# First 1/rms by ln and exp on ScalarE, squares shared with GpSimd, 128-column score weights, first projections in parts, last store split

## Chip, cores, metric

One core of one Trainium2 chip. The metric is the device time of one execution in microseconds (us). Several executions are taken of each kernel. "Clock" is the mean TensorE clock that the throttle granted, with 1.0 as full speed.

## The reference

Attention with normalised q and k, then a gated two-layer projection (shapes: 8 batches, 12 heads, 448 positions, head size 64; model width 768, hidden width 2048):

```python
def rmsnorm(x, g):
    rms = np.sqrt(np.mean(x * x, axis=-1, keepdims=True) + 1e-06)
    return x / rms * g
q_n, k_n = rmsnorm(q, g_q), rmsnorm(k, g_k)
scores = scale * np.matmul(q_n, k_n.transpose(0, 1, 3, 2))     # then softmax
attn_out = np.matmul(attn, v)
x = attn_out.transpose(0, 2, 1, 3).reshape(B * S, H * D)
h = x @ w_in
out = (h * (1.0 / (1.0 + np.exp(-1.702 * h)))) @ w_out
```

## The kernel before

Heads go in 48 pairs. A pair is loaded, squared (ACT), summed (DVE), given 1/rms (a bit-trick seed and two Newton steps), multiplied by it ("norm"), turned on PE, copied out of PSUM by DVE, scored in four chunks, exponentiated (ACT), multiplied with v on PE, divided (DVE), turned back and copied to `xt`. Six pairs make one batch's input of the first projection. A list scheduler written into the kernel emits the instructions; where it sees PE idle early on, it emits filler matmuls on zeros, meant to keep the clock up (before's trace shows full clock from 6.6 us, where its record of the clock begins, to 443.5). Each engine then runs its own list in that order, so an instruction waits behind whatever stands before it (on PE a transposition of pair 6 waits for GpSimd until 47.69 us, and pair 5's values, whose last exponential ended at 45.22, follow at 47.90).

```python
groups = [[0], [1, 2], [3, 4, 5]] + [list(range(j, j + 3)) for j in range(NP, NG, 3)]
def fill(idle):
    for _ in range(int(idle * FILL / 110)):
        nc.tensor.matmul(banks[2][:, :256], lhsT=ident[:, :], rhs=zeros[:, :], start=True, stop=True)
def square(i, part):
    ...
    nc.scalar.activation(out=sq_of[i][:SS, part], in_=raw[i][:SS, part], func=ACT.Square)
def rsqrt(grp):
    eng = nc.vector if grp[0] == 0 else nc.gpsimd
    ...                                   # two Newton steps
def norm(i, gi):
    eng = nc.vector if i == 0 else nc.gpsimd
    ...
def score(i, kcs):
    for kc in kcs:
        ...
            nc.tensor.matmul(sc[:SS, hp, :S], lhsT=qk_ring[i % N_KZ][r, 1, kc, :],   # 112 columns
                             rhs=qk_ring[i % N_KZ][r, 0], start=True, stop=True)
def first(b, m):                          # waits for all six pairs of the batch
    ...
    for ki in range(KI):
        nc.tensor.matmul(ps, lhsT=w_in_s[:, ki, m * 128:(m + 1) * 128],
                         rhs=xT[b][:, ki, :], start=(ki == 0), stop=(ki == KI - 1))
```

Of the kernel before, what the change touches and what calls it, by code (L numbers as in the profile page):

```python
# [19 lines left out]
class _Task:  # L20
    __slots__ = ("eng", "dur", "lat", "emit", "key", "after", "at", "takes", "left", "users", "end", "start", "lock", "widen", "moves", "rest", "there")


class _Order:
# [3 lines left out]
    def __init__(self):  # L28
        self.tasks = []
        self.named = {}  # L30
        self.slots = {}
        self.fill = None

# [3 lines left out]
    def add(self, name, eng, dur, emit, key, deps=(), lat=100.0, at=0.0, takes=None,  # L37
            lock=False, widen=None, moves=None):

        t = _Task()  # L40
        t.eng, t.dur, t.lat, t.emit = eng, dur, lat, emit
        t.after, t.at, t.takes = tuple(deps), AT.get(name, at), takes
        t.users, t.end, t.lock, t.widen = [], None, lock, widen
        t.moves = moves
        t.key = KEYS.get(name, key)
        self.tasks.append(t)
        self.named[name] = t

    def run(self):
# [53 lines left out]
        while emitted < len(self.tasks):  # L103
            for eng, q in ready.items():
                while q and free[eng] <= now:
# [12 lines left out]
                    if best.takes:  # L118
                        self.slots[best.takes[0]][1].extend(best.takes[1])
# [13 lines left out]
                    if best.moves:  # L133
                        best.rest, best.there, best.end = best.moves, free[eng] + 1500.0, 1e12
# [30 lines left out]

    def _fits(self, t, now):
# [3 lines left out]
        if not t.takes:  # L170
            return True
        n, held = self.slots[t.takes[0]]
# [9 lines left out]
KEYS = {  # L182
    ('V', 6): 2.73, ('KQ', 4): 2.03, ('O', 6, 0): 3.05, ('O', 6, 1): 3.05, ('N', 6, 0): 1.73,
    ('N', 6, 1): -2.28, ('Q0', 5): 5.11, ('X', 5): 3.87, ('O', 4, 0): 10.58, ('O', 4, 1): 10.58,
    ('V', 9): -3.51, ('B', 4): 5.7, ('N', 8, 0): 9.82, ('N', 8, 1): 17.49, ('R', 7, 0): -27.36,
    ('C', 5, 0): -2.3, ('C', 5, 1): -2.05, ('C', 5, 2): -1.8, ('C', 5, 3): -1.55, ('C', 0, 0):
    7.52, ('C', 0, 1): 7.77, ('C', 0, 2): 8.02, ('C', 0, 3): 8.27, ('X', 7): 22.5, ('E', 9, 0):
    1.77, ('E', 9, 1): 2.02, ('E', 9, 2): 2.27, ('E', 9, 3): 2.52, ('E', 8, 0): 9.55, ('E', 8,
    1): 9.8, ('E', 8, 2): 10.05, ('E', 8, 3): 10.3, ('L', 4, 0): -3.71, ('L', 4, 1): -1.78,
    ('L', 4, 2): 3.79, 'gG': 2.03, ('L', 6, 0): 16.21, ('L', 6, 1): 16.04, ('L', 6, 2): 15.02,  # L190
    ('V', 4): 11.79, ('X', 2): 31.45, ('KQ', 6): 7.83, ('O', 2, 0): 1.7, ('O', 2, 1): 1.7, ('O',
    3, 0): 5.2, ('O', 3, 1): 5.2, ('V', 5): -21.45, ('T', 1, 0): -1.19, ('T', 1, 1): -1.19,
    ('B', 8): 8.59, ('K', 0): -8.3, ('P', 8, 0, 0): 6.19, ('P', 8, 0, 1): 6.31, ('P', 8, 0, 2):
    6.44, ('P', 8, 0, 3): 6.56, ('P', 8, 1, 0): 6.69, ('P', 8, 1, 1): 6.81, ('P', 8, 1, 2):
    6.94, ('P', 8, 1, 3): 7.06, ('P', 3, 0, 0): 10.39, ('P', 3, 0, 1): 10.51, ('P', 3, 0, 2):
    10.64, ('P', 3, 0, 3): 10.76, ('P', 3, 1, 0): 10.89, ('P', 3, 1, 1): 11.01, ('P', 3, 1, 2):
    11.14, ('P', 3, 1, 3): 11.26, ('S', 1, 0): -4.92, ('S', 1, 1): -4.92, ('O', 0, 0): -14.63,
    ('O', 0, 1): -14.63, ('X', 0): 0.11, ('R', 2, 0): -12.65, ('B', 6): -4.39, ('B', 0): 6.44,
    ('WI', 1): -46.42, ('T', 6, 0): -14.6, ('T', 6, 1): -14.6, ('KQ', 7): 8.67, ('N', 7, 0):
    0.23, ('N', 7, 1): 0.86, ('WI', 2): -48.21, ('P', 9, 0, 0): 1.73, ('P', 9, 0, 1): 1.85,  # L200
    ('P', 9, 0, 2): 1.98, ('P', 9, 0, 3): 2.1, ('P', 9, 1, 0): 2.23, ('P', 9, 1, 1): 2.35, ('P',
    9, 1, 2): 2.48, ('P', 9, 1, 3): 2.6, ('Q0', 8): 26.56, ('L', 9, 0): 1.37, ('L', 9, 1): 2,
    ('L', 9, 2): 2.03, ('S', 2, 0): 3.28, ('WO', 0): -62.3, ('S', 7, 0): -6.72, ('K', 6): 8.9,
    ('V', 2): 6.1, ('C', 9, 0): 8.24, ('C', 9, 2): 8.74, ('E', 0, 0): 7.69, ('E', 0, 1): 7.94,
    ('E', 0, 2): 8.19, ('E', 0, 3): 8.44, ('R', 3, 0): -4.24, ('K', 3): 15.15, ('K', 4): -25.1,
    ('B', 7): 15.31, ('WI', 3): -42.16, ('T', 9, 0): 1.28, ('T', 9, 1): 1.28, ('E', 5, 0):
    12.03, ('E', 5, 1): 12.28, ('E', 5, 2): 12.53, ('E', 5, 3): 12.78, ('B', 1): -1.87, ('E', 7,
    0): 28.17, ('E', 7, 1): 28.42, ('E', 7, 2): 28.67, ('E', 7, 3): 28.92, ('K', 8): 47.59,
    ('L', 0, 0): -11.05, ('L', 0, 1): -11.4, ('L', 0, 2): -7.53, ('N', 3, 0): -16.28, ('N', 3,
    1): -14.36, ('K', 2): -16.75, ('Q', 0): -4.76, ('Q', 2): -5.74, ('KQ', 0): -29.98, ('T', 3,  # L210
    0): -12.32, ('T', 3, 1): -12.32, ('P', 6, 0, 0): 3.39, ('P', 6, 0, 1): 3.51, ('P', 6, 0, 2):
    3.64, ('P', 6, 0, 3): 3.76, ('P', 6, 1, 0): 3.89, ('P', 6, 1, 1): 4.01, ('P', 6, 1, 2):
    4.14, ('P', 6, 1, 3): 4.26, ('R', 9, 0): 25.96, ('T', 0, 0): 0.39, ('T', 0, 1): 0.39, ('B',
    5): 2.45, ('S', 8, 0): 3.96, ('O', 5, 0): -1.87, ('O', 5, 1): -1.87, ('N', 9, 1): -9.18,
    ('K', 9): 3.37, ('E', 6, 0): 19.35, ('E', 6, 1): 19.6, ('E', 6, 2): 19.85, ('E', 6, 3):
    20.1, ('N', 0, 0): -4.14, ('N', 0, 1): -1.78, ('S', 4, 0): -31.05, ('O', 1, 0): -5.09, ('O',
    1, 1): -5.09, ('N', 1, 0): -9.91, ('N', 1, 1): -1.76, ('V', 7): -0.09, ('KQ', 3): -10.96,
    ('N', 9, 0): -5.62, ('L', 7, 1): -15.12, ('T', 8, 0): 3.81, ('T', 8, 1): 3.81, ('V', 8):
    4.32, ('E', 2, 0): -5.17, ('E', 2, 1): -4.92, ('E', 2, 2): -4.67, ('E', 2, 3): -4.42, ('R',
    4, 0): 6.71, ('R', 6, 0): -1.32, ('P', 5, 0, 0): 16.5, ('P', 5, 0, 1): 16.62, ('P', 5, 0,  # L220
    2): 16.75, ('P', 5, 0, 3): 16.87, ('P', 5, 1, 0): 17, ('P', 5, 1, 1): 17.12, ('P', 5, 1, 2):
    17.25, ('P', 5, 1, 3): 17.37, ('WO', 1): -77.76, ('S', 5, 0): -1.79, ('V', 1): 4.46, ('S',
    0, 0): -28.66, ('S', 0, 1): -28.66, ('B', 2): 9.79, ('Q0', 2): -3.7, ('P', 2, 0, 0): 5.38,
    ('P', 2, 0, 1): 5.51, ('P', 2, 0, 2): 5.63, ('P', 2, 0, 3): 5.76, ('P', 2, 1, 0): 5.88,
    ('P', 2, 1, 1): 6.01, ('P', 2, 1, 2): 6.13, ('P', 2, 1, 3): 6.26, ('K', 1): 5.11, ('KQ', 5):
    -13.6, ('E', 4, 0): -6.4, ('E', 4, 1): -6.15, ('E', 4, 2): -5.9, ('E', 4, 3): -5.65, ('N',
    4, 0): -13.48, ('N', 4, 1): -11.01, ('P', 1, 0, 0): 25.19, ('P', 1, 0, 1): 25.32, ('P', 1,
    0, 2): 25.44, ('P', 1, 0, 3): 25.57, ('P', 1, 1, 0): 25.69, ('P', 1, 1, 1): 25.82, ('P', 1,
    1, 2): 25.94, ('P', 1, 1, 3): 26.07, ('N', 2, 0): 5.89, ('N', 2, 1): 6.22, ('S', 3, 0):
    -13.09, ('R', 5, 0): 13.51, ('S', 9, 0): -6.12, ('KQ', 8): -5.51, ('P', 7, 0, 0): 19.18,  # L230
    ('P', 7, 0, 1): 19.31, ('P', 7, 0, 2): 19.43, ('P', 7, 0, 3): 19.56, ('P', 7, 1, 0): 19.68,
    ('P', 7, 1, 1): 19.81, ('P', 7, 1, 2): 19.93, ('P', 7, 1, 3): 20.06, ('X', 4): 4.14, ('R',
    0, 0): -18.6, ('R', 0, 1): -18.6, ('Q', 8): -19.17, ('B', 9): 2.73, ('E', 1, 0): -9.59,
    ('E', 1, 1): -9.34, ('E', 1, 2): -9.09, ('E', 1, 3): -8.84, ('T', 4, 0): 15.41, ('T', 4, 1):
    15.41, ('WO', 3): -23.99, ('C', 1, 0): -11.21, ('C', 1, 1): -10.96, ('C', 1, 2): -10.71,
    ('C', 1, 3): -10.46, ('L', 5, 0): 3.49, ('L', 5, 1): 4.35, ('L', 5, 2): -1.58, ('Q', 5):
    -7.85, ('X', 1): -14.02, ('T', 2, 0): 0.05, ('T', 2, 1): 0.05, ('C', 6, 0): 3.8, ('C', 6,
    2): 4.3, ('K', 5): -7.73, ('K', 7): -10.83, ('Q0', 0): -13.4, ('KQ', 1): -28.02, ('X', 9):
    -9.97, ('N', 5, 0): 8.49, ('N', 5, 1): 10.13, ('T', 5, 0): 15.04, ('T', 5, 1): 15.04, ('O',
    8, 0): 20.07, ('O', 8, 1): 20.07, ('V', 3): -0.2, ('C', 8, 0): 8.01, ('C', 8, 2): 8.51,  # L240
    ('L', 7, 0): -16.71, ('L', 7, 2): -14.17, ('S', 6, 0): -1.89, ('L', 2, 0): -13.69, ('L', 2,
    1): -12.03, ('L', 2, 2): -10.74, ('L', 8, 0): 3.25, ('L', 8, 1): 8.83, ('L', 8, 2): 15.6,
# [27 lines left out]
def kernel(  # L270
# [37 lines left out]
    zeros = consts.tile([128, 256], BF16)  # L308
    nc.vector.memset(zeros[:, :], 0.0)
    ones = consts.tile([128, 1], FP32)  # L310
    nc.vector.memset(ones[:, :], 1.0)


    gq = consts.tile([128, 1], FP32)
# [325 lines left out]
    def first(b, m):  # L640
        if b == m == 0:
            order.insert(0, 2)
# [123 lines left out]
```

## Time and profile before

| | before |
|---|---|
| median, 3 runs | 448.08 us (447.36 to 448.12) |
| profiled span, clock | 446.0 us, 0.997 |
| first exponential starts, 24th ends | 16.40, 45.22 us |
| first projection starts | 50.77 us |
| last matmul ends | 440.74 us |

A line of a timeline gives start, length, engine, source line, operation, tiles, and in brackets how long the engine was idle before it and what released it. The prediction below shows the lines that carry the argument. One more belongs here, the VectorE timeline where pair 0 is normed:

```profile
13.03 0.69 DVE L439 TENSOR_TENSOR row<-raw,rs 112x512 bf16<-112x512 f32 x1
```

One norm takes 0.69 us on DVE (the other 0.68).

### The profile page before, as it was taken

The page shows a single profiled execution, that of the slowest core. Times are in us where ns is not written, and L with a number is a line of the kernel's source. Part 1 is how long each engine was busy: PE and PEld are TensorE (multiplying, and loading weights), DVE is VectorE, ACT ScalarE, POOL GpSimd, SP SyncE. Part 2 cuts the span into 40 slices and gives each one's busy share as a digit, 9 for nine tenths or more (in the row PEclk, how much of TensorE's full clock was granted, in tenths as well). Part 3 has the DMA queues.
Part 4 walks back from the last instruction along what each step waited for, and adds up shares of the span by engine and source line. Part 5 has one row for each costly group of instructions (what it writes and reads, how often), then busy time and mean ns, then how long its engine had stood idle before and what let it go on. Part 6 is the DMA issues. An engine that isn't in the chain of part 4 may idle for free.

```text
span 446.0 us, 9981 instructions
## 1 busy us (share of the span) xinstructions
PE 437.9 (98%) x3955; PEld 259.2 (58%) x3955; DVE 214.3 (48%) x458; ACT 319.0 (72%) x463; POOL 184.8 (41%) x285
## 2 busy tenths in 40 slices
PE   8999999999999999999999999999999999999995
PEld 6767655665556555565556555565555555565552
DVE  3778777664763347633762256612541125404400
ACT  4689588898998878977887788866876667414311
POOL 1775985656646453544643635455242100000000
PEclk9999999999999999999999999999999999999998
DMA  7999999959556775397456684445123430121022
GB/s 205 274 235 245 262 249 241 225 149 223 149 141 156 189 196 151 83 210 189 122 137 155 178 208 114 125 109 135 32 57 74 105 77 12 22 71 37 0 72 71
DMA packets 97391, 63.38 MB, mean 142 GB/s; under 512 B 54336, under 2 KB 93760, under 8 KB 97344
## 3 DMA queue, kind: packets, MB, share of 16 engines
q1 hardware_dynamic: 89488, 56.22, 50.2%
q0 software_dynamic: 7296, 6.29, 8.7%
q8 instruction: 31, 0.51, 0.5%
q10 hardware_dynamic: 560, 0.23, 0.2%
q14 instruction: 16, 0.13, 0.1%
HBM read 45.61 MB, written 11.01 MB: 127 GB/s over the span
## 4 chain that ended last, share of the span: by engine, by line
PE 87%; DMA 7%; POOL 2%; DVE 2%; SPq 0%; issue 0%; ACT 0%; ACTq 0%; POOLq 0%; DVEq 0%
PE w L668 33%; PE w L645 32%; PE o L498 11%; PE sc L487 9%; DMA raw<-in_q_dram 5%; POOL row L439 1%; DMA gq<-in_g_q_dram 1%; DMA vraw<-in_v_dram 1%; PE w L459 1%; DVE ssq L401 1%; POOL w_in_s L619 0%; PE w L521 0%; SPq L390 0%; DVE rs L414 0%; DVE g L660 0%
## 5 line engine op out<-in xcount | busy, mean ns | idle before, releaser
L491 ACT ACTIVATE att<-sc 112x896 bf16<-112x896 f32 x192 | 167.9, 916 | 22.1 <-PE sc L487 20.9
L668 PE MATMUL w<-w_out_s,g 128*128 128x384 bf16 x896 | 161.6, 326 | 0.0
L645 PE MATMUL w<-xt,w_in_s 128*128 128x448 bf16 x768 | 158.4, 352 | 0.4 <-DVE g L660 0.2
L668 PEld LDWEIGHTS <-g 128*128 128x128 bf16 x896 | 80.3, 97 | 50.9 <-issue 5.7
L660 DVE SCALAR_TENSOR_TENSOR g<-th,w 128x448 bf16<-128x448 f32 x128 | 78.9, 618 | 63.9 <-ACT th L654 63.6
L645 PEld LDWEIGHTS <-w_in_s 128*128 128x128 bf16 x768 | 69.5, 97 | 57.5 <-issue 2.1
L439 POOL TENSOR_TENSOR row<-raw,rs 112x512 bf16<-112x512 f32 x94 | 96.0, 1044 | 16.4 <-DMA qk<-row 14.7
L498 PEld LDWEIGHTS <-att 112*128 112x128 bf16 x1536 | 73.7, 98 | 45.0 <-issue 21.1
L654 ACT ACTIVATE th<-w 128x448 f32<-128x448 f32 x128 | 69.8, 545 | 36.8 <-PE w L645 35.4
L449 POOL TENSOR_TENSOR vx<-vraw,ones 112x512 bf16<-112x512 f32 x42 | 43.7, 1042 | 113.8 <-PE o L498 106.6
L498 PE MATMUL o<-vx,att 112*128 112x65 bf16 x1536 | 87.4, 194 | 0.2 <-DVE obs L509 0.2
L401 DVE TENSOR_REDUCE ssq<-sq 112x16 f32<-112x1024 f32 (+1 forms) x50 | 58.5, 1174 | 28.9 <-ACT sq L395 27.7
L508 DVE RECIPROCAL rcp<-o 112x4 f32<-112x4 f32 x96 | 17.3, 180 | 97.9 <-PE o L498 97.3
L678 ACT ACTIVATE osb<-w 128x384 f32<-128x384 f32 x56 | 27.5, 490 | 50.9 <-PE w L668 49.2
L487 PE MATMUL sc<-qk 64*112 64x448 bf16 x384 | 57.9, 373 | 0.3 <-DVE qk L466 0.2
L395 ACT ACTIVATE sq<-raw 112x1024 f32<-112x1024 f32 (+1 forms) x50 | 51.1, 1023 | 8.9 <-DMA raw<-in_k_dram 8.1
L509 DVE TENSOR_TENSOR obs<-o,rcp 112x256 bf16<-112x256 f32 x96 | 40.7, 424 | 3.3
L369 PE MATMUL w<-zeros,ident 128*128 128x256 bf16 x227 | 32.5, 288 | 1.4 <-POOL ident masks.py:199 1.4
L487 PEld LDWEIGHTS <-qk 64*112 64x112 bf16 x384 | 17.8, 124 | 16.3 <-issue 11.2
L369 PEld LDWEIGHTS <-ident 128*128 128x128 bf16 x227 | 21.7, 103 | 7.0 <-issue 2.3
L477 ACT ACTIVATE qk<-qk,gG 128x448 bf16<-128x448 bf16 x36 | 24.2, 672 | 0.0
L425 POOL TENSOR_TENSOR t<-rs 112x48 f32<-112x48 f32 (+1 forms) x32 | 8.8, 275 | 33.8 <-DVE rs L414 31.1
(32 smaller groups left out, 89.9 us busy)
## 6 DMA issues: line engine op xcount, KB each, us to landing
raw<-in_q_dram SPq DMA_DIRECT2D x48, 224.0 KB, 4.1
vraw<-in_v_dram SPq DMA_DIRECT2D x48, 224.0 KB, 3.9
raw<-in_k_dram SPq DMA_DIRECT2D x47, 224.0 KB, 4.3
w_in_s<-in_moe_w_in_dram POOLq DMA_DIRECT2D x4, 768.0 KB, 14.3
w_out_s<-in_moe_w_out_dram POOLq DMA_DIRECT2D x4, 768.0 KB, 15.7
out_dram<-osb SPq DMA_DIRECT2D x8, 336.0 KB, 3.0
out_dram<-osb SPq DMA_DIRECT2D x8, 288.0 KB, 2.8
out_dram<-osb SPq DMA_DIRECT2D x8, 240.0 KB, 3.3
```

The lines of the kernel that those rows point to most:

```text
L369: nc.tensor.matmul(banks[2][:, :256], lhsT=ident[:, :], rhs=zeros[:, :], start=True, stop=True)
L395: nc.scalar.activation(out=sq_of[i][:SS, part], in_=raw[i][:SS, part], func=ACT.Square)
L401: nc.vector.reduce_sum(out=ssq_of[g0][:SS, i - g0, part], in_=sq_of[i][:SS, part], axis=AX.X)
L439: eng.tensor_tensor(out=row_ring[i % N_QKN][:SS, gi].rearrange("p n (h d) -> p h n d", h=2), in0=raw[i][:SS, gi], in1=y[:SS, a, gi].to_bro ...
L449: nc.gpsimd.tensor_tensor(out=vx[:, :, :D], in0=vr, in1=ones[:SS, :].to_broadcast([SS, 2 * NS, D]), op=ALU.mult)
L487: nc.tensor.matmul(sc[:SS, hp, :S], lhsT=qk_ring[i % N_KZ][r, 1, kc, :], rhs=qk_ring[i % N_KZ][r, 0], start=True, stop=True)
L491: nc.scalar.activation(out=att_ring[i % N_ATT][:SS, kc, :, :S], in_=scs.pop((i, kc))[:SS, :, :S], func=ACT.Exp)
L498: nc.tensor.matmul(os_[i, hp][:, qs, :], lhsT=att_ring[i % N_ATT][:SS, kc, hp, qs * SS:qs * SS + WIN], rhs=vx_ring[i % N_V][:SS, hp, kc, : ...
L645: nc.tensor.matmul(ps, lhsT=w_in_s[:, ki, m * 128:(m + 1) * 128], rhs=xT[b][:, ki, :], start=(ki == 0), stop=(ki == KI - 1))
L654: nc.scalar.activation(out=th[:, :], in_=gps[b, m], func=ACT.Tanh, scale=0.851)
L660: nc.vector.scalar_tensor_tensor(out=g_of[b // 2][:, m, lo:lo + S], in0=ths.pop((b, m))[:, :], scalar=1.0, in1=gps.pop((b, m)), op0=ALU.ad ...
L668: nc.tensor.matmul(ops[bp, tm, hf], lhsT=g_of[bp][:, ko, tm * 128:(tm + 1) * 128], rhs=w_out_s[:, ko, hf * HALF:(hf + 1) * HALF], start=(k ...
```

## The change

The intent: get the attention of the first six pairs out sooner, by taking the Newton steps off DVE and GpSimd (ln and exp on ACT need two short instructions), moving some squares from ACT to GpSimd, and beginning the first two projections with the pairs that are ready; and shorten the dense stage with 128-column score weights. Its core, with cuts; the scheduler's priorities were redrawn as well, and buffers became fixed rings:

```diff
 def square(i, part):
+    if ("S", i, part.start) in ON:
+        nc.gpsimd.tensor_tensor(out=sq[i % N_SQ][:SS, part], in0=raw[...], in1=raw[...], op=ALU.mult)
+        return
...
+def by_log(i):                            # pairs 0 to 5
+    nc.scalar.activation(out=x, in_=x, func=ACT.Ln, bias=eps[:SS, :])
+    nc.scalar.activation(out=y[:SS], in_=x, func=ACT.Exp, scale=-0.5)
...
-    nc.tensor.matmul(sc[:SS, hp, :S], lhsT=qk_ring[i % N_KZ][r, 1, kc, :],
+    k0 = S + kc * SS
+    nc.tensor.matmul(sc[:, hp, :S], lhsT=qkw_ring[i % N_KZ][r, k0:k0 + WIN],      # WIN = 128
...
-def first(b, m):
+def first(b, m, kis):
...
+    parts = [range(KI - 2), [KI - 2], [KI - 1]] if b == 0 and m < 2 else [range(KI)]
...
-    for lo in (0, 64):                    # g loads: from ACT's queue to SP's
-        nc.scalar.dma_start(out=t[lo:lo + 64, :], in_=src.rearrange("(d o) -> d o", o=1))
+    nc.sync.dma_start(out=t[:, :], in_=src.rearrange("(x d o) -> x d o", x=1, o=1).to_broadcast([2, D, 1]))
...
+    for j, eng in enumerate((nc.scalar, nc.vector)):     # the last tile: halves, stores on two queues
```

## The prediction

> **What bounds the kernel now.** I read the page first: engine shares, the slices, then the costliest groups. Lines from the page (engine, busy time; then group: line, engine, operation, busy us, mean ns, idle before):
>
> ```profile
> PE 437.9 (98%) x3955; PEld 259.2 (58%) x3955; DVE 214.3 (48%) x458; ACT 319.0 (72%) x463; POOL 184.8 (41%) x285
> DMA  7999999959556775397456684445123430121022
> ...
> L491 ACT ACTIVATE att<-sc 112x896 bf16<-112x896 f32 x192 | 167.9, 916 | 22.1 <-PE sc L487 20.9
> ...
> L369 PE MATMUL w<-zeros,ident 128*128 128x256 bf16 x227 | 32.5, 288 | 1.4 <-POOL ident masks.py:199 1.4
> L487 PEld LDWEIGHTS <-qk 64*112 64x112 bf16 x384 | 17.8, 124 | 16.3 <-issue 11.2
> L498 PEld LDWEIGHTS <-att 112*128 112x128 bf16 x1536 | 73.7, 98 | 45.0 <-issue 21.1
> ```
>
> PE looks full, but 227 of its matmuls are fillers on zeros (L369). The PE timeline shows where they sit: all are before the first projection (L645) at 50.77 us. The windows view split at that moment and at the last matmul gives:
>
> ```profile
> 0.00:50.77 50.77, 48.48 (x560) 35.59 (x560) 34.43 (x85) 33.77 (x40) 30.74 (x60) 1.00 1.07 241
> 50.77:440.76 389.99, 389.39 (x3398) 223.61 (x3396) 179.89 (x374) 284.71 (x423) 154.06 (x226) 1.00 0.54 130
> ```
>
> So there are two stages. After 50.77 PE is busy 389.4 of 390.0 us with real work: only less PE work can shorten it. Before 50.77, PE waits for the first six head pairs, and ACT sets the pace. The ACT and PE timelines (start, length, engine, what, count):
>
> ```profile
> 1.36 12.97 PE L369 MATMUL w<-zeros,ident 128*128 128x256 bf16 x94 [1.36 <-POOL ident masks.py:199]
> 16.40 0.92 ACT L491 ACTIVATE att<-sc 112x896 bf16<-112x896 f32 x1 [1.79 <-PE sc L487]
> 26.91 3.34 ACT L491 ACTIVATE att<-sc 112x896 bf16<-112x896 f32 x4 [0.40 <-PE sc L487]
> 44.26 0.96 ACT L491 ACTIVATE att<-sc 112x896 bf16<-112x896 f32 x1
> 47.69 0.37 PE L459 MATMUL w<-ident,row 112*128 112x112 bf16 x4 [0.67 <-POOL row L439]
> ```
>
> The first exponential starts at 16.40, the 24th (six pairs, four each) ends at 45.22. These 28.8 us are 24 x 0.835 (3.34/4) = 20.0, seven squares at a pitch of 0.945 = 6.6, and 2.1 of small waits. Then 5.6 us pass to the first projection, partly because a transposition of pair 6 stands in PE's order ahead of pair 5's values and waits for GpSimd until 47.69.
>
> PE time without use before 50.77: 1.36 at the start; 94 fillers up to 14.17 us, 12.8; 133 more x 0.107 = 14.2; idle 1.1. Sum **29.5 us**; so 21.3 us was useful.
>
> [...] 112 columns load in 124 ns, 128 columns in 98, with 112 rows or 128. [...] Here 94 fillers take 12.8 us; at 0.107 they would take 10.0, so some 26 ran at 0.213. [...] The one load here took 1283 ns[...]. [...] Here the 112x512 product takes 1044 ns on POOL, 683 on DVE.
>
> **The change, part by part.** Counts are from the instruction order of the built program.
>
> *1/rms of pairs 0 to 5.* Removed on DVE for pair 0: two seed and six Newton instructions, 8.26 to 9.90 = 1.6 us, with three reductions ahead of the first norm (9.82 to 12.2). Removed on POOL: 16 small instructions for pairs 1 to 5, 13.2 to 16.2 and 23.1 to 26.2, together 6 us, and the wait of a pair for its group. Added on ACT: a ln and an exp of 16 columns per pair. [...] Two pairs are before the first exponential, four after.
>
> *Squares.* Of the squares of full or half pairs, POOL takes two halves (1.04 each) and those of pairs 3, 6, 7, 9, 10, 11 (about 2.1 each). Between first and 24th exponential ACT keeps three squares, 3 x 0.945 = 2.8, instead of seven.
>
> *First exponential.* 57 fillers now precede the first transposition: 26 x 0.213 + 31 x 0.107 = 8.9, so PE is free at 10.2. Pair 0's loads land at about 6 to 6.5 (5.2 and 5.8 before; they now stand behind one more load and the two small g loads); square 0.63, reduction 0.68[...], two norms 1.3: about 10.3. Transposition, copies (0.39 + 0.45), score and semaphores took 2.2 us before (14.16 to 16.40). First exponential: about **12.2** instead of 16.4.
>
> *The 24th.* 20.0 + 2.8[...] + the same 2.1 of waits = 27.1, so 39.3 instead of 45.2.
>
> *First projections in parts.* Ten of the first 12 matmuls (0.19 each) now run before pair 5 is done; after the last exponential come values, division, values, division, transposition, copy: about 4.0 us to the end of the first projection. Useful PE work up to there is the six pairs (48 transpositions at 0.049, 24 scores at 0.33, 48 value groups at 0.13, 6 transpositions back: 17.7) plus 2.3 of projection plus the same 2.4 of switching: 22.4. Time without use: 39.3 + 4.0 - 22.4 = **20.9**.
>
> *The same by counting fillers.* 138 instead of 227: 1.36 + 8.9 + 81 x 0.107 (8.7) + idle. After the first projection begins no filler is placed, and the order shows five waits for DVE round trips (two of about 0.9, the others 0.3 to 0.7), so I take 3 us of idle: **22**. Both ways: 29.5 falls by 7.5 to 8.6. I take **7.8**.
>
> *Score weights.* 84 double steps (four loads each) lie in the dense stage. Each load is 124 - 98 = 26 ns shorter, but loads partly lie beside matmuls. One to two of four exposed: 84 x 0.026 to 0.052 = 2.2 to 4.4. A single look at such a step: second pair of matmuls 0.23 after the first, next operation 0.28 later, where streaming alone is two times 0.187. I take **2.5**.
>
> *Last store.* Before, the last 384 columns leave PSUM in 0.49, then two stores are issued one after the other (0.45 each) from SP. Now half the bytes, issued from two queues: minus 0.45 and an estimated 0.5 of transfer; but the order shows DVE's part waiting for ACT's: plus 0.25. **0.7** saved.
>
> *Neutral.* Free choice of PSUM bank and fixed rings: in the dense stage PE waited 0.4 us in all, so nothing is to be had. The second table load (1.28) follows the 24th exponential and lies under the 4 us of values and divisions.
>
> Sum: 7.8 + 2.5 + 0.7 = 11.0; 448.1 - 11.0 = **437.1**, say 437.0.
>
> **Rivals.** *DMA becomes the bound of the start.* For: its slices are full from 11 to 89 us, and single loads took 8.35 and 12.87 us from issue to landing while weights moved; now three of four input weight chunks are asked for before pair 3 is normed, and two output chunks before pair 4 is. If pair 4 or 5 lands 3 us late, the time is 440. Against: pair 5's last load is the 20th of its queue; twenty of 229 KB at the 247 GB/s of this stretch (0.93 us each) and two or three chunks at 4.9 (8.7% of the span for eight) make some 30 us, and pair 5 is needed at about 26 to 28 us: near need, so not excluded. *GpSimd becomes the bound.* Pair 2's rows stand behind a 2.1 us square; if its lane stalls the exponentials, 1 to 2 us are lost: 438.5. Against: it loses 6 us of Newton steps and gains about as much. *The start is gained but refunded later*: if a gap in the dense stage opens because ACT or POOL is late, the gain shrinks to 6 or 7: 441. Against: ACT is busy 285 of 390 there and POOL 154. *Everything lands*: exposed weight loads at two per step and no idle after the first projection: 433.
>
> **Range and chances.** Main uncertainty: idle in the first 45 us, about 2.5 us either way; weight loads 1 us. Range 433 to 441.5. The 2% line is at 439.1, some 0.8 of my spread away, and a DMA wait is the one likely way across it: faster 0.72, same 0.26, slower 0.02.
>
> **What would show it.** Right: first exponential near 12.2, 24th ends near 39.3, first projection whole near 43, time without use near 21.5; weight loads of scores near 98 ns and the dense PE work 2.5 us shorter; span after the last matmul 4.5 instead of 5.2. Wrong: raw loads of pairs 2 to 5 as the releasers of ACT's squares with long waits; PE idle of over 4 us after the first projection has begun; score steps as long as before in spite of shorter loads; releasers from GpSimd in the dense stage.

Passages of the prediction are cut. With them goes the term for ln and exp, which stood in two sums: 10.3 us for pair 0's norms and 27.1 from the first exponential to the end of the 24th are the sums as recorded, with that term in them, and so are 12.2, 39.3, 20.9 and 437.1, which follow from them. (A ln and an exp took 0.30 and 0.22 us in the changed kernel's trace, started 0.33 apart.) The 0.5 of transfer in the last store's term is the author's estimate; the page of before has a median of 3.0 us from issue to landing for stores of 336 KB and 2.7 for those of 192 KB.

## The result

After: 440.15 us (median of 4 runs, 439.37 to 441.26) against 447.79 for before on the same chip. Ratio 0.983, 95% interval 0.981 to 0.986. The gain is 7.6 us where 11 was predicted, inside the predicted range but 3.1 us above its centre, and on the "within 2%" side of the line.

The page of the changed kernel: engine shares, the granted clock and the DMA share in 40 slices, then the costliest groups.

```profile
PE 428.7 (98%) x3866; PEld 244.6 (56%) x3866; DVE 216.2 (49%) x452; ACT 316.3 (72%) x468; POOL 191.2 (44%) x277
PEclk9899899999999999999999999999999999999999
DMA  7999999594699974677547774655133430121022
...
L433 PE MATMUL w<-zeros,ident 128*128 128x256 bf16 x138 | 22.6, 305 | 1.4 <-POOL ident masks.py:199 1.4
L558 PEld LDWEIGHTS <-qk 64*128 64x128 bf16 x384 | 11.8, 94 | 19.4 <-issue 14.6
```

Score weights now load in 94 ns instead of 124, and there are 138 fillers instead of 227. But the clock row has two eights, in the slices from 11 and from 44 us. Splitting the start where the clock changes gives the windows view (stretch, its length, then busy us and count of PE, weight loads, DVE, ACT, POOL; then clock, DMA share and GB/s):

```profile
0.00:13.24 13.24, 9.54 (x64) 7.25 (x65) 5.68 (x12) 4.54 (x8) 6.59 (x21) 1.00 0.80 203
13.24:16.65 3.41, 3.27 (x19) 1.66 (x19) 1.66 (x3) 0.94 (x2) 3.14 (x3) 0.50 1.11 272
16.65:40.36 23.71, 23.71 (x312) 15.36 (x313) 17.61 (x42) 22.45 (x32) 17.91 (x17) 1.00 1.17 248
40.36:47.34 6.98, 4.65 (x68) 3.06 (x67) 5.34 (x13) 3.11 (x4) 3.80 (x11) 1.00 1.19 246
47.34:50.75 3.41, 3.30 (x9) 1.32 (x9) 1.20 (x3) 1.10 (x3) 3.41 (x4) 0.50 1.22 249
50.75:435.07 384.32, 384.18 (x3398) 216.00 (x3396) 184.35 (x381) 283.83 (x421) 156.35 (x226) 1.00 0.56 133
```

TensorE ran at half speed in two stretches of 3.41 us each, 34.1 us (ten times 3.41) apart. (The 1.00 of the first row holds only from 6.4 us on: the trace records no clock before that, and there the fillers follow each other at 0.213 us instead of 0.107.) Each stretch follows a time in which PE was partly idle. Ahead of the first these were the waits for pair 0, in the PE timeline:

```profile
11.63 0.37 PE L529 MATMUL w<-ident,row 112*128 112x112 bf16 x4 [1.43 <-DVE row L509]
...
13.38 0.53 PE L529 MATMUL w<-ident,row 112*128 112x112 bf16 x4 [1.05 <-DVE qk L533]
```

Before has no such stretch from 8 to 20 or from 40 to 55 us. The dense stage is full, as before: 384.18 of 384.32 us busy.

Pair 0's first steps, from the ACT timeline, then the loads that SP issued:

```profile
7.98 0.63 ACT L458 ACTIVATE sq<-raw 112x512 f32<-112x512 f32 x1 [5.97 <-DMA raw<-in_q_dram]
...
15.71 0.92 ACT L562 ACTIVATE att<-sc 112x896 bf16<-112x896 f32 x1 [2.91 <-PE sc L558]
...
40.46 1.73 ACT L562 ACTIVATE att<-sc 112x896 bf16<-112x896 f32 x2
42.21 1.28 ACT L356 ACT_TABLE_LOAD   x1
```

```profile
0.73 0.39 SPq L451 DMA_DIRECT2D raw<-in_q_dram  x1
1.18 0.72 SPq L608 DMA_DIRECT2D gq<-in_g_q_dram  x1
1.95 0.54 SPq L608 DMA_DIRECT2D gk<-in_g_k_dram  x1
2.53 2.03 SPq L451 DMA_DIRECT2D raw<-in_q_dram  x2
```

Pair 2's q goes first, then both g; pair 0's q is in the pair of loads that took 2.03 us to issue (the single load ahead of them took 0.39, the g loads 0.72 and 0.54), and ACT waits for it until 7.98. The first exponential starts at 15.71, hardly earlier than the 16.40 of before. The 24th ends at 42.19, followed by the table load. Then the VectorE and GpSimd timelines around pair 0's norms:

```profile
10.43 2.59 DVE L509 TENSOR_TENSOR row<-raw,rs 112x512 bf16<-112x512 f32 x2
```

```profile
9.99 1.04 POOL L519 TENSOR_TENSOR vx<-vraw,ones 112x512 bf16<-112x512 f32 x1 [1.69 <-DVE ssq L467]
11.18 2.74 POOL L509 TENSOR_TENSOR row<-raw,rs 112x512 bf16<-112x512 f32 x2 [0.15 <-ACT rs L479]
```

Two norms took 2.59 us on DVE, where two of 0.68 would make 1.36, while GpSimd worked beside them and needed 2.74 for two of its own norms (2.04 in experiments 2, 5 and 12, where it did them after DVE's). Last, the PE timeline after the first parts of the projections:

```profile
43.56 0.37 PE L590 MATMUL w<-ident,obs 112*128 112x112 bf16 x4 [0.99 <-DVE obs L578]
...
45.17 0.68 PE L569 MATMUL o<-vx,att 112*128 112x65 bf16 x16 [0.23 <-DVE obs L578]
46.60 0.37 PE L590 MATMUL w<-ident,obs 112*128 112x112 bf16 x4 [0.74 <-DVE obs L578]
47.45 4.43 PE L725 MATMUL w<-xt,w_in_s 128*128 128x448 bf16 x14 [0.48 <-DVE xt L593]
```

Four waits for DVE, 2.4 us together, with no filler in them; then 14 projection matmuls take 4.43 us at half clock where 14 of 0.19 are 2.7. And the chain of waits that ended last runs through this place so (start, length, what):

```profile
39.63 0.95 ACT sq L458
40.61 2.35 DVE ssq L467 x2
...
43.08 0.44 DVE obs L578
```

The chain isn't that of the last exponentials: it comes from the square of a later pair on ACT (itself behind earlier exponentials), two reductions of later pairs on DVE, and only then pair 4's second division.

The last matmul ends at 435.07 in a span of 439.5: 4.43 us of tail against 5.26 before.

So between the two profiled runs the last matmul moved by 440.74 - 435.07 = 5.67 us and the tail by 0.83. As experiment 9 measures the score weights at 2.7, some 3.0 us are left for the start, where 7.8 was predicted. The question for the experiments is where the other 4.8 went.

### The profile page after: what moved, and what is told of

Same layout as the page of the kernel before. It is cut to its first block, busy times and chain, and to the rows that moved or that the text cites. A ratio compares the mean times of both kernels' runs of the same rounds, so it can differ in the third digit from the quotient of the medians.

```text
span 439.5 us, 9799 instructions
## 1 busy us (share of the span) xinstructions
PE 428.7 (98%) x3866; PEld 244.6 (56%) x3866; DVE 216.2 (49%) x452; ACT 316.3 (72%) x468; POOL 191.2 (44%) x277
## 4 chain that ended last, share of the span: by engine, by line
PE 94%; DVE 2%; DMA 1%; ACT 1%; SPq 1%; issue 0%
PE w L748 34%; PE w L725 33%; PE o L569 12%; PE sc L558 11%; PE w L433 2%; PE w L529 1%; DVE ssq L467 1%; DMA raw<-in_q_dram 1%; PE w L590 1%; SPq L451 0%; ACT att L562 0%; ACT sq L458 0%; DVE row L509 0%; DVE obs L578 0%; SPq L608 0%
## 5 line engine op out<-in xcount | busy, mean ns | idle before, releaser
L509 POOL TENSOR_TENSOR row<-raw,rs 112x512 bf16<-112x512 f32 x90 | 92.8, 1054 | 26.7 <-DMA qk<-row 19.7
L569 PEld LDWEIGHTS <-att 112*128 112x128 bf16 x1536 | 70.9, 98 | 42.8 <-issue 21.2
L569 PE MATMUL o<-vx,att 112*128 112x65 bf16 x1536 | 83.8, 194 | 0.2 <-DVE obs L578 0.2
L467 DVE TENSOR_REDUCE ssq<-sq 112x16 f32<-112x1024 f32 (+1 forms) x50 | 58.1, 1171 | 20.9 <-ACT sq L458 20.8
L558 PE MATMUL sc<-qk 64*128 64x448 bf16 x384 | 55.3, 357 | 0.1
L458 ACT ACTIVATE sq<-raw 112x1024 f32<-112x1024 f32 (+1 forms) x42 | 43.3, 1034 | 7.1 <-DMA raw<-in_q_dram 6.0
L433 PE MATMUL w<-zeros,ident 128*128 128x256 bf16 x138 | 22.6, 305 | 1.4 <-POOL ident masks.py:199 1.4
L558 PEld LDWEIGHTS <-qk 64*128 64x128 bf16 x384 | 11.8, 94 | 19.4 <-issue 14.6
L433 PEld LDWEIGHTS <-ident 128*128 128x128 bf16 x138 | 13.5, 109 | 7.0 <-issue 3.1
L455 POOL TENSOR_TENSOR sq<-raw 112x1024 f32<-112x1024 f32 (+1 forms) x8 | 13.3, 1678 | 6.6 <-DMA raw<-in_k_dram 2.5
```

What stands on the lines that cost most here:

```text
L458: nc.scalar.activation(out=sq[i % N_SQ][:SS, part], in_=raw[i % N_RAW][:SS, part], func=ACT.Square)
L467: nc.vector.reduce_sum(out=ssq_of[g0][:SS, i - g0, part], in_=sq[i % N_SQ][:SS, part], axis=AX.X)
L509: eng.tensor_tensor(out=row_ring[i % N_QKN][:SS, gi].rearrange("p n (h d) -> p h n d", h=2), in0=raw[i % N_RAW][:SS, gi], in1=y[:SS, a, gi ...
L558: nc.tensor.matmul(sc[:, hp, :S], lhsT=qkw_ring[i % N_KZ][r, k0:k0 + WIN], rhs=qk_ring[i % N_KZ][r, 0], start=True, stop=True)
L569: nc.tensor.matmul(os_[i, hp][:, qs, :], lhsT=att_ring[i % N_ATT][:SS, kc, hp, qs * SS:qs * SS + WIN], rhs=vx_ring[i % N_V][:SS, hp, kc, : ...
```

## The experiments

Times are medians. Experiments 1 to 4 shared one set of runs of before (447.67), 5 to 8 another (447.6), 9 to 12 a third (447.91). Where a run is compared with one of another set (5, 7, 8 and 10 with 3, 11 with 1), the difference of the ratios to before gives the same within 0.2 us.

**1. The changed kernel once more, unedited.** It measures how far it repeats.

> The changed kernel once more, unedited, as the base for this chip. Expected 440 us (ratio 0.983 to the kernel before), with a spread of about 2 us from run to run, and in its trace again half-clock stretches near 14 and 47 us. If the half-clock stretches are an accident of the one profiled run, they are missing here.

440.86 us (439.32 to 442.04, 5 runs), ratio 0.984. A stretch of 3.41 us at half speed lowers the mean clock by 3.41 x 0.5 / 440 = 0.0039, so the mean clock counts the stretches of a run, but roughly: the clock can also fall after the last matmul (in before's trace from 443.5 us on, which alone makes its 0.997). Of the nine runs of the changed kernel, five have clock 0.992, two stretches, and take 441.2 us in the mean; four have 0.994 to 0.996, about one, and take 439.7. The spread of 2.7 us follows this count. This run's own trace has the two again, at 13.64 and 47.77, once more 34.1 apart.

**2. Fillers in the four waits after the 24th exponential**, 20 in all, that add zero to the open projection:

```diff
+def warm(n):
+    for _ in range(n):
+        nc.tensor.matmul(gps[0, 0][:, :256], lhsT=ident[:, :], rhs=zeros[:, :], start=False, stop=False)
 def values(i, hp, qs):
+    if (i, hp, qs) == (5, 1, 0): warm(2)
 def back_pe(i):
+    if i in (4, 5): warm(8 if i == 4 else 6)
 ...                                       # and warm(4) ahead of the first projection's last part
```

> 20 matmuls on zeros, which add nothing, are put into the four waits of TensorE between the first part of the first projection and its last part. Clock theory: the granted clock stays 1.00 from 40 to 52 us, the 14 projection matmuls at 47.5 us take 2.7 us instead of 4.4, and the kernel gets 1.5 to 1.8 us faster than the unedited one, in those runs that had the drop. Rival (only the DVE round trips bound this stretch, the drop is harmless): same time within 0.4 us.

440.73 us (437.67 to 441.33), ratio 0.983. The one traced run had no half-clock stretch (clock 0.999), its 14 projection matmuls took 2.93 us, and it was the fastest, 437.67. The four others had 0.992 to 0.994 and were no faster than without the fillers. They have no trace, so where they lost their clock isn't known. Nor does the traced run owe its lead to the fillers alone: pair 0's norms, which come before them, took 1.28 there, and the first exponential started at 13.52. By itself this run settles nothing.

**3. Fillers also before pair 0's two transpositions**, where PE waited 1.43 and 1.05 us:

```diff
 def turn_pe(i, gi):
+    if i == 0:
+        for _ in range(12 if gi == 0 else 10):
+            nc.tensor.matmul(banks[2][:, :256], lhsT=ident[:, :], rhs=zeros[:, :], start=True, stop=True)
```

> As the one before, and 22 more matmuls on zeros ahead of the first two transpositions, at 10.2 to 13.4 us. Clock theory: no half clock near 14 to 17 us, the first exponential starts at about 14.9 instead of 15.7, and a further 0.5 to 0.8 us is gained. Rival (ACT is then bound by other waits, so the start of the first exponential does not matter): first exponential earlier, time the same as the one before within 0.3 us. If the fillers delay the transpositions, it is slower.

438.45 us (438.26 to 438.80), ratio 0.980, clock 0.999 or 1.0 in all four runs, and the spread fell to 0.5 us. Mean against mean of experiment 1: 440.79 - 438.49 = **2.3 us**. Work was added and the kernel became faster; the waits themselves didn't go away, PE only does something in them. In the trace the 14 projection matmuls take 2.93 us and no stretch is at half clock. DVE's six norm products took 960 ns in the mean in this trace, 1044 in that of experiment 1, so not all of the difference between the two traced runs is the clock's; experiment 11 is the cleaner pair.

**4. The changed kernel with score weights in 112 columns again.**

```diff
-nc.tensor.matmul(sc[:, hp, :S], lhsT=qkw_ring[i % N_KZ][r, k0:k0 + WIN],
+nc.tensor.matmul(sc[:SS, hp, :S], lhsT=qkw_ring[i % N_KZ][r, k0:k0 + SS],
```

> The changed kernel with 112 score weight columns again, in the same order. From the accounts of both traces the 128 columns are worth 3.3 us (84 steps of 0.04 us), so 3.3 us slower than the unedited one; the prediction's term was 2.5; if the loads were hidden, no change. Weight loads of scores near 124 ns instead of 94, a double score step 0.52 us instead of 0.48 to 0.49.

443.76 us (441.33 to 444.76, 6 runs), ratio 0.991 against 0.984 with 128: 2.9 us. The clock varied from 0.99 to 0.999, so the number is rough; experiment 9 takes the same thing at a steady clock.

**5. On top of 3, pair 0's loads first:** pair 0's q ahead of pair 1's and 2's, the g loads after them, the product of the g behind pair 0's norms; fewer fillers at the start, as the wait is shorter.

```diff
 def load(i, which):                       # cut: pair 2's and 1's q are held back until pair 0's and 1's are out
+    if (i, which) == (0, 0): load(1, 0)
+    if (i, which) == (1, 1): load(2, 0); load_g_now()
 def take_k(i):
+    if i == 0: scale_g_now()
```

> The kernel with both gaps kept busy (ratio 0.9796, 438.45 us), with pair 0's q load first in the SP queue, pair 1's next, pair 2's q and the two g loads after them, the g product moved behind the first norm, and fewer fillers at the start so that they do not stand in the way. Theory (the late landing of pair 0's q, 7.9 us instead of the predicted 6 to 6.5, is the largest term of the late start): q lands at 5 us, first exponential at 11.5 to 12 instead of 14.4, and the whole gets 2 to 2.7 us faster. Rival (pair 2's data or another lane then holds ACT up, and the gain is lost before the 24th exponential): first exponential earlier, time gains under 1 us.

437.81 us (437.42 to 438.42), ratio 0.978. On ACT (timeline):

```profile
11.84 1.06 ACT L471 ACTIVATE sq<-raw 112x1024 f32<-112x1024 f32 x1 [2.93 <-DMA raw<-in_k_dram]
12.81 0.90 ACT L581 ACTIVATE att<-sc 112x896 bf16<-112x896 f32 x1
```

Pair 0's q lands at 4.3 instead of 8, and the norms, now ahead of most of GpSimd's work, take 1.28 for two. But pair 2's square stands ahead of the first exponential in ACT's list and waits for its k, so the exponential starts at 12.81 and not at 11.6. The 24th ends at 39.07 instead of 40.48: 1.4 us earlier, of which only 0.6 reach the end (ratio 0.978 against 0.980, with intervals that overlap). The chain of waits tells why:

```profile
21.90 15.53 DMA raw<-in_k_dram
...
37.58 1.90 POOL sq L468
...
39.51 1.22 DVE ssq L480
...
40.85 0.42 DVE obs L604
```

A k of a later pair, 15.53 us under way, lands at 37.4; GpSimd squares it, DVE sums it, and pair 4's division stands behind that sum in DVE's list. The end of the first stage is held by a transfer, for which starting earlier does nothing.

**6. Pair 1's norms and pair 2's copy of v from GpSimd to DVE, and the first weight load later**, to leave DVE alone during pair 0's norms.

```diff
-eng = nc.vector if (i == 0) != (("N", i, gi) in ON) else nc.gpsimd
+eng = nc.vector if (i <= 1) != (("N", i, gi) in ON) else nc.gpsimd
```

> The kernel with both gaps kept busy, with pair 1's two norms and pair 2's copy of v on DVE behind pair 0's norms, so that GpSimd does nothing while DVE norms pair 0 (the first weight load is asked for behind the square of pair 3, some 2 us later than before). Theory (the two norms of pair 0 take 2.1 to 2.6 us instead of 1.36 because GpSimd works beside them): norms at 0.68 us each, first exponential at 13.4 to 13.7, whole 0.7 to 0.9 us faster. Rival (norms are slow for another reason, as the wait for data): norms stay at 1.1 to 1.3 us each. A further rival: with pair 1's norms on DVE the later scores come late and take the gain back.

The result was wrong (relative error 0.20): my deferred copy of pair 2's v stood behind the load that refills its buffer, and DVE waited for that load. The time, 445.83, says nothing. One line before the fault is usable, from the DVE timeline, with GpSimd idle beside it:

```profile
10.48 1.28 DVE L511 TENSOR_TENSOR row<-raw,rs 112x512 bf16<-112x512 f32 x2
```

1.28 again, against 2.59 in the changed kernel. In the traces of experiments 2, 5, 6 and 7 GpSimd was idle during all or most of the two norms, and they took 1.28. In those of the changed kernel and experiments 3 and 8 GpSimd worked beside them, and they took 2.59, 2.13 and 2.34.

**7. On top of 3, ln and exp replaced by a seed and two Newton steps on DVE for each early pair** (cut; eight instructions, pair 1's behind pair 0's norms).

```diff
-nc.scalar.activation(out=x, in_=x, func=ACT.Ln, bias=eps[:SS, :])
-nc.scalar.activation(out=y[:SS], in_=x, func=ACT.Exp, scale=-0.5)
+nc.vector.tensor_scalar(...)              # two for the seed, then twice three for Newton
```

> The kernel with both gaps kept busy, but 1/rms of pairs 0 to 5 by the seed and two Newton steps on DVE, one pair at a time (pair 1's behind pair 0's norms), no ln and exp on ACT and no second table load. DVE pays 1.64 us for each pair. Theory (ACT's work between first and 24th exponential sets the pace): first exponential 1.1 us later, the stretch of 24 exponentials 2.1 us shorter, whole 0.5 to 1 us faster than with ln and exp. Rival (DVE's chain sets the pace as well): the stretch does not shrink and the whole is 1 to 2 us slower.

450.44 us, ratio 1.006: 12 us slower than 3. I had held that ACT alone sets the pace, so that work taken off it could only help; that fell. ACT now waits for scores:

```profile
16.56 2.56 ACT L580 ACTIVATE att<-sc 112x896 bf16<-112x896 f32 x3 [4.22 <-PE sc L576]
22.23 1.87 ACT L580 ACTIVATE att<-sc 112x896 bf16<-112x896 f32 x2 [3.11 <-PE sc L576]
```

The size isn't to be read as the worth of ln and exp: the order was planned for them and was not planned anew.

**8. On top of 3, all squares back on ACT.** (`("S", i, part.start) in ON` becomes `False`.)

> The kernel with both gaps kept busy, with all squares back on ACT. ACT gets three more full squares (pairs 3, 6, 7) of 0.945 us between first and 24th exponential, and two halves of 0.63 before. Theory: the 24th exponential ends 2.8 to 3.4 us later and the whole is 2.8 to 3.4 us slower. Rival (ACT has slack there, or GpSimd's squares slow DVE as much as they save): under 1.5 us slower.

440.38 us (439.81 to 440.45), clock 1.0: 1.9 us slower than 3. The 24th exponential ends at 42.67 instead of 40.48. So the moved squares are worth 1.9 us here, less than the 2.8 to 3.4 expected, and the prologue of this kernel is set by ACT to that extent.

**9. The kernel before with 128-column score weights alone.** The edit is the score line of the diff above, with the wider buffer that it needs.

> The kernel before with one thing of the change: score weights in 128 columns. Theory (read off the pair of runs with and without it on the changed kernel, 2.9 us): weight loads of scores near 98 ns instead of 124, double score steps near 0.485 us instead of 0.52, and the whole 2.5 to 3.3 us faster than before, ratio 0.9925 to 0.9945; the first exponential stays at 16.4 and the first projection near 50.8, because ACT sets the pace there. Rival (the score step only shows the saving when the rest of the change is there): within 1 us of before, ratio over 0.9975.

445.11 us (444.92 to 445.24), ratio 0.994, interval 0.993 to 0.995: 447.9 x 0.006 = **2.7 us**. Its score weights load in 94 ns. The first exponential stays at 16.27: the part works by itself.

**10. On top of 3, the first two projections undivided**, with fillers in the place of their first parts.

```diff
+if b == 0 and m < 2:
+    if kis[-1] < KI - 1:                  # cut: 7 or 2 fillers instead of this part
+        return
+    kis = range(KI)
```

> The version with fillers before the first transpositions and in the four gaps, but the first two projections undivided, with fillers where their first parts stood, so that the clock stays up. Ten real matmuls of 0.19 us then come after pair 5 is done. Theory: 1.9 us slower than the same version with the parts (438.45), so 440.3, ratio to before 0.983 to 0.985, clock 0.998 or more. Rival (PE has room for them later, or the fillers there cost as much): under 0.8 us slower.

440.27 us (439.96 to 440.63), ratio 0.983 against 0.980: 1.7 us slower, near the ten matmuls of 0.19 that it moves behind the wait. In its trace, though, the first exponential starts at 15.10 instead of 14.39 and the 24th ends at 41.20, 0.7 us later than in 3, so the 1.7 may not be the parts' alone. It leaves one thing untried: pair 4's second values stand behind those early matmuls on PE, and the fillers here keep that place occupied.

**11. The changed kernel with the fillers of 3 at the start only.**

> The changed kernel with fillers only before pair 0's two transpositions (12 and 10), none in the four gaps after the 24th exponential. It tells which waits of PE the lost clock comes from. Theory A (both places count alike, each costs its own half-clock stretch): clock 0.994 to 0.996 in most runs, a stretch at half speed near 47 us and none near 14 us, whole time 439.5 to 440.3. Theory B (only the waits at the start decide[...]): clock 0.999 in all runs and 438.2 to 438.8, as with fillers in both places. Theory C (neither): 440.8.

438.70 us (438.28 to 440.60, 5 runs), ratio 0.981, clock 0.996 to 1.0. Mean 439.03, 1.8 us less than the unedited kernel (1.6 by the ratios), so most of the 2.3 comes with the 22 fillers at the start. The traced run shows no half-clock stretch from 8 to 20 or from 40 to 55 us, although the four waits are all still there:

```profile
42.09 0.37 PE L594 MATMUL w<-ident,obs 112*128 112x112 bf16 x4 [0.99 <-DVE obs L582]
...
45.13 0.37 PE L594 MATMUL w<-ident,obs 112*128 112x112 bf16 x4 [0.74 <-DVE obs L582]
45.98 2.93 PE L729 MATMUL w<-xt,w_in_s 128*128 128x448 bf16 x14 [0.48 <-DVE xt L597]
```

The same waits cost a stretch in one run and none in another. This pair of traces also prices a stretch, as the norms were alike (DVE's six norm products 1026 ns in the mean here, 1036 in the changed kernel). The runs differ by 3.0 us (438.28 and 441.26): the 24th exponential ends at 40.73 instead of 42.19, and the 14 matmuls take 2.93 instead of 4.43. That is about 1.5 us for each stretch, as in the nine runs of experiment 1 (441.2 and 439.7).

**12. On top of 5, pair 2's square behind the first exponential**, its ln and exp behind the third, its sum behind pair 1's copies.

```diff
 def expo(i, kc):
+    if (i, kc) == (0, 0): square_now(2, slice(0, 2))
+    if (i, kc) == (0, 2): by_log_now(2)
```

> The best version so far (fillers in both places, pair 0's loads first, pair 2's and the g loads later: 437.81) and one thing more: pair 2's square, which held the first exponential back from 11.6 to 12.81 while it waited for pair 2's k, stands behind the first exponential on ACT, its ln and exp behind the third, its reduction on DVE behind pair 1's copies. Theory (every microsecond that ACT begins earlier comes out at the end): first exponential 11.6, 24th ends 37.9 to 38.4, whole 436.9 to 437.3. Rival (ACT idles later instead, since pair 2's norms come later or DVE and GpSimd cannot keep up): first exponential 11.6, 24th ends 38.8 or later, whole 437.5 or more.

437.44 us (436.74 to 439.90, 5 runs), ratio 0.9785 against 0.9782 for 5. The first exponential starts at 11.68, 1.1 us earlier, as meant; nothing of it reaches the mean. In the traced run, the slowest, it went as the rival has it: the last two of the 24 exponentials run from 37.81 to 39.52, later than in 5. That trace shows more, first on GpSimd, then on PE:

```profile
38.73 1.89 POOL L475 TENSOR_TENSOR sq<-raw 112x1024 f32<-112x1024 f32 x1 [3.65 <-DMA raw<-in_k_dram]
```

```profile
42.48 0.37 PE L645 MATMUL w<-ident,obs 112*128 112x112 bf16 x4 [2.05 <-DVE obs L631]
```

GpSimd waits 3.65 us for the same kind of late k, pair 4's division slips to 42.0, PE idles 2.05 us, and a half-clock stretch follows from 44.0 to 47.4. Two of the five runs have clock 0.994 or 0.995 and take 439.4 to 439.9; the three others 436.7 to 437.4, about where the theory put them, and they have no trace. So whether the earlier start pays in a run without a stretch stays open. Version 5 is the steadier one: 437.8 us, 2.2% less than before, within 1.0 us in all its runs; by time the two can't be told apart.

## Why the prediction was right or wrong

- **The odds.** A gain of more than 2% had 0.72, and a DMA wait was named as the one likely way to miss it. The gain was 1.7%; with the stretches at half clock away (experiment 3) it was 2.0%, and no rival named the clock. That the time still lies in the range is partly luck: its width was meant for idle time and weight loads.
- **Two stages, the dense one bound by PE.** Right: PE is busy 384.18 of 384.32 us there, and no wait was refunded into it.
- **Score weights, 2.5.** Right: 2.7 (experiment 9), 2.9 (experiment 4, rough).
- **Last store, 0.7.** About right: 0.83 from the tails of the two profiled runs, not tested alone.
- **ln and exp.** Measured: 0.30 for ln, 0.22 for exp, started 0.33 apart, so 0.55 us a pair.
- **From the first exponential to the end of the 24th, 27.1.** Right: 42.19 - 15.71 = 26.5.
- **Neutral parts.** The second table load (1.28 us from 42.21 us) lies beside DVE's sums and pair 4's division (40.61 to 43.5), as said.
- **The start, 7.8.** This is the term that was mis-sized: about 3.0 measured. Its steps:
  1. "First exponential: about 12.2." It was 15.71. The sum itself has slips: from 6 to 6.5 us its terms, with the measured 0.55 for ln and exp, lead to 9.2 to 9.7, not 10.3, and 10.3 + 2.2 is 12.5. Besides, three terms were too small. The loads of pair 0 were taken as landed at 6 to 6.5 and landed at 8 (issued behind the g loads, in 2.03 us). "Two norms 1.3" took 2.59 beside GpSimd. And transposition, copies and scores were taken at "2.2" at full clock, but ran inside a half-clock stretch (13.24 to 16.65). With loads in order, the first exponential came at 12.81, and with pair 2's square out of its way at 11.68.
  2. "After the last exponential ... about 4.0." It took 5.26 until the first projection's last part began. The step assumed that only pair 5's own steps follow. The kernel has one PSUM buffer for these values, so pair 4's second values and division come first; and the chain of waits goes to those through the square and two sums of later pairs, not through the last exponential.
  3. "Idle of 3 us" after the first projection had begun was near (2.4 us in four waits before its last part), but its price was not: in this trace 3.41 us at half clock came after it, in which the 14 matmuls took 1.5 us longer (4.43 against 2.93 in experiment 11). The prediction counted idle time as lost once and the fillers as mere waste. This is the largest missing term: 2.3 us with both places (experiment 3).
- **Adding up.** From 437.0 to 440.15 are 3.15 us. The clock accounts for 2.3, the order of the loads with its effect on the norms for 0.6 at the end (experiment 5), the two better terms for -0.3; some 0.5 remain, for which step 2 is the candidate. That remainder is argued, not shown.
- **The rivals.** DMA was not the bound of the changed kernel, as held. In the traces of experiments 5 and 12, where the start was faster, a late k holds the end of the first stage: the gains of 1.4 and 1.1 us on ACT shrank to 0.6 and, in the mean of all runs, nothing. GpSimd as the bound: not as meant, but beside its work two norms on DVE took 2.59 us instead of 1.28. Refunds in the dense stage: none.

Why fillers at the start alone mostly suffice, the traces answer in part. In those of the changed kernel and experiment 1 the two half-clock stretches of 3.41 us lie ten times 3.41 us apart (13.24 and 47.34; 13.64 and 47.77), and the last change of the first trace, at 439.89, another 115 times: in each trace the clock changes on a grid of 3.41 us, and where it lies differs from run to run. From 8 to 20 and from 40 to 55 us experiment 4 has one stretch, from 13.38, and experiment 12 one, from 44.05. Add up PE's idle time in each step of this grid at full clock, within the same two windows. The six steps ahead of a stretch have 2.3 and 1.4 us (the changed kernel), 2.3 and 1.4 (experiment 1), 2.35 (experiment 4) and 1.9 (experiment 12); in the changed kernel no single wait among them is longer than 1.43. Four other steps of these traces have 0.8 to 1.1 us, and no stretch follows. So in these traces a stretch goes with the idle time of a whole step, and several short waits are enough. Where the grid lies in experiment 11, whose four waits no stretch follows, was not shown, and what decides between 1.1 and 1.4 us stays open.

Open too: what is left if the sums of later pairs leave DVE's list ahead of pair 4's divisions. By itself it may be little: in the trace of the changed kernel pair 4's second values end on PE at 42.57, only 0.3 us before their division can start on DVE at 42.87, because they stand behind eight early projection matmuls (40.36 to 41.89).

## What to carry to other kernels

Before removing filler work, ask what it was for: here 1.4 to 2.35 us of idle PE time within 3.41 us cost the idle time and, in some runs, half of the next 3.41 us; the spread from run to run together with the mean clock revealed it (2.7 us at 0.992 to 0.996, 0.5 us at 0.999 to 1.0 with the fillers of experiment 3). When a wait is shortened at the head of a chain, look along the chain of waits for the in-order lists and the transfers that will hold its later links, because the gain stops at the first that didn't move (in experiment 5, 0.6 of 1.4 us reached the end). And give the first item's loads the head of the queue, ahead of even the smallest others (pair 0's q landed at 4.3 us instead of 8).
